# First loads, exponentials by bank and the order of the last tiles in a gated linear-attention and feed-forward kernel

The change has three parts: small loads leave the software DMA queue and the gate column is made by a TensorE transpose; exponentials are done one PSUM bank at a time in the tiles that have little other work behind them; the last tiles are ordered and placed in PSUM differently.

## The chip, the cores and the metric

One core of one Trainium2 chip. The metric is the device time of one execution in microseconds (us). A profile gives the span between first and last instruction, about 2 us less than the time. PE is TensorE's matmul stream, PEld its weight loads, DVE VectorE, ACT ScalarE, POOL GpSimd and SP SyncE; a "q" after a name is its sequencer or DMA queue.

## The reference

```python
# x: [1, 2048, 512] bf16; 32 heads of 16; Dff = 1376
g = sigmoid((x * gate_w).sum(-1, keepdims=True))
q, k, v = heads(x @ wqkv)
pq, pk  = q @ w_phi, k @ w_phi                      # per head, 16 x 16
phi_q   = [softmax(pq), softmax(-pq)]               # 32 features a head; phi_k likewise
kv, z   = phi_k^T v, sum_s phi_k
a       = concat_heads((phi_q kv) / (phi_q z + 1e-6)) @ wo
b       = relu(x @ w1) @ w2
return g * a + (1 - g) * b
```

(B_x is not used; both halves read A_x.)

## The kernel before

A small planner records each engine's instructions with events and turns the events into semaphore waits, so every engine runs in the order of the plan. 16 tiles of 128 rows of x; "H units" are four matmuls each of x @ w1 (128 columns of w1 by 512 rows of x). The loads, in SP's order, and the five small loads on GpSimd's software queue:

```python
for i in range(2):
    p.dma("sp", ... XS[:, 2*i:2*i+2, :] <- xq ...)           # x0i, 256 KB
    load_w1(i)                                               # w10, w11: columns 0..511, 128 KB each
load_w1(2); load_w1(3)                                       # w12, w13
p.dma("sp", ... W1[:, :, 512:DFF] <- B_w1 ...)               # w1r, "the remainder of W1", 864 KB
p.dma("sp", ... WV ...)                                      # 512 KB
p.dma("sp", ... WQKT, transposing ...)                       # wqk, 1 MB
...                                                          # x1..x3, transposing
p.dma("pool", ... WPS <- A_w_phi ...)
for dt in range(NDT):                                        # gate_w as column 1376 of W1
    p.dma("pool", ... W1[:, dt, DFF:DFF+1] <- gate_w ...)
```

The gate's logit is one more output row of the last H unit (`KT - 1`), so that unit needs the gate column. The first units work on w10 to w13; from the fifth on they wait for the remainder. Then come the weight products (`pre`: wqk times the block-diagonal `Wbd`, which DVE builds from w_phi), then the tiles:

```python
def atile(m):        # Q and K features into PSUM banks 0 and 1, then the exponentials
    first = xready(m // 4) + ([f"em{m-1}"] if m else [pc0..pc7])     # both banks read by ACT
    for dt in range(NDT):
        for which, W in ((0, WqP), (1, WkP)): matmul(PS[:, which, :], ...)
    for s, nm in ((0, "ep"), (1, "em")):                             # lastq: by bank
        act(exp, out 128x1024, in PS[:, 0:2, :], scale=+-1)
    ...
nh = [2, 2, 2, 2, 2, 1, 2, 2, 1, 2, 2, 1, 3, 2, 2]                   # H units behind each tile

def nd(m):           # numerators: two banks, 0,1 or 4,5; then divide and DMA-transpose into OT
def finB(m):         # relu(h) @ w2, eleven matmuls, banks 2, 3, 7
def finA(m):         # OT @ wo, four matmuls, bank 6, scaled by g on ACT
...
nd(0); hnext(); gate(); finB(1)
nd(1)
for m in range(NT - 1):
    if m + 2 < NT: nd(m + 2)
    finA(m); comb(m)
    if m + 2 < NT: finB(m + 2)
last(NT - 1)         # tile 15 in two halves
```

The softmax here doesn't subtract the row's maximum and nothing guards it: scores larger than these inputs give would overflow.

## Time and profile before

| | us |
|---|---|
| time, median of three runs | 156.34 (155.41 to 156.79) |
| time, median of six runs, three of them beside the changed kernel | 156.09 (154.95 to 159.93) |
| span of the profiled run | 153.7 |
| PE busy | 146.7 of it (95%), 928 matmuls |
| first H unit on the remainder starts | 10.56 |
| projections of tile 0 start | 20.30 |
| first combine of the last tile, after PE's last matmul slot | 0.73 |

A profile is read here by asking where PE's stream has a hole and what ended it. In the "chain that ended last" each row is start, duration and what; "issue" is time in which the profile shows nothing to wait for. A row of "waits" gives who waited <- for whom, us in all, times, longest. The slot of a 512-column matmul is 0.216 us in this trace; where starts lie further apart there is a hole. The lines are in the prediction.

### The profile page before, as it was taken

The numbers are of one execution on the slowest core, as the hardware profiler recorded it, in microseconds if no ns is written. First come the engines' busy times: TensorE is split into PE (matmuls) and PEld (weight loads), VectorE is DVE, ScalarE is ACT, GpSimd is POOL, SyncE is SP. The second block draws the span as 40 slices with busy tenths as digits, with TensorE's granted clock in tenths as the row PEclk, the third lists the DMA queues.
The fourth block names the chain that finished last, engine by engine and source line by source line (L and its number), as shares of the span: only waits on it lengthen the run. The fifth ranks groups of instructions, "written<-read, shape, count | busy, mean of one in ns | idle before, by whom it ended". The sixth has DMA issues, their size and how long they took to land.

```text
span 153.7 us, 2371 instructions
## 1 busy us (share of the span) xinstructions
PE 146.7 (95%) x928; PEld 72.8 (47%) x928; DVE 90.0 (59%) x147; ACT 79.2 (52%) x122; POOL 55.4 (36%) x62
## 2 busy tenths in 40 slices
PE   5979999999999999999999999999999999999990
PEld 1834644444445444444544445444444444544450
DVE  1600546777668876866868788564545544455523
ACT  3357749788777877887787773111221111111131
POOL 8100007778866866878686653000000000000000
PEclk9999999999999999999999999999999999999999
DMA  4799992963433331533333311433222233233222
GB/s 165 193 320 259 156 237 53 374 145 73 68 68 68 70 61 35 47 68 70 68 75 68 68 27 41 102 72 103 68 68 73 69 87 83 68 93 82 68 68 68
DMA packets 41178, 15.57 MB, mean 101 GB/s; under 512 B 36704, under 2 KB 40432, under 8 KB 41168
## 3 DMA queue, kind: packets, MB, share of 16 engines
q1 hardware_dynamic: 40336, 13.47, 39.7%
q0 software_dynamic: 688, 1.95, 3.9%
q8 instruction: 7, 0.11, 0.3%
q14 instruction: 3, 0.02, 0.1%
q10 hardware_dynamic: 144, 0.01, 0.0%
HBM read 4.41 MB, written 2.10 MB: 42 GB/s over the span
## 4 chain that ended last, share of the span: by engine, by line
PE 82%; DMA 8%; ACT 5%; SPq 2%; DVE 1%; issue 1%; DVEq 0%
PE PS L452 22%; PE PS L257 21%; PE PS L306 18%; PE PS L461 8%; PE PS L359 7%; DMA W<-in_B_w_dram 5%; ACT FM L316 4%; DMA OT<-OTM 4%; PE PS L422 2%; PE PS L381 2%; PE PS L286 1%; SPq L139 1%; SPq L150 1%; ACT TFA L466 0%; ACT HT L272 0%
## 5 line engine op out<-in xcount | busy, mean ns | idle before, releaser
L452 PE MATMUL PS<-W,HT 128*128 128x512 bf16 (+1 forms) x176 | 40.6, 379 | 0.0
L257 PE MATMUL PS<-XT,W 128*128 128x512 bf16 (+1 forms) x160 | 38.0, 379 | 1.0 <-DMA W<-in_B_w_dram 1.0
L316 ACT ACTIVATE FM<-PS 128x1024 bf16<-128x1024 f32 x30 | 29.1, 1021 | 14.3 <-PE PS L306 14.3
L342 POOL TENSOR_TENSOR FM<-FM,SC 128x1024 bf16<-128x1024 bf16 x15 | 29.0, 1930 | 15.1 <-DVE SC L327 15.1
L466 ACT ACTIVATE TFA<-PS,GT 128x512 bf16<-128x512 f32 x15 | 10.3, 688 | 42.9 <-PE PS L461 42.9
L324 DVE TENSOR_REDUCE ZB<-FM 128x64 f32<-128x1024 bf16 x16 | 19.5, 1220 | 19.0 <-ACT FM L316 18.6
L272 ACT ACTIVATE HT<-PS 128x512 bf16<-128x512 f32 (+1 forms) x44 | 24.8, 605 | 8.0 <-PE PS L257 5.1
L452 PEld LDWEIGHTS PS<-W,HT 128*128 128x128 bf16 (+1 forms) x176 | 17.2, 98 | 20.8
L306 PE MATMUL PS<-WqP,XT 128*128 128x512 bf16 x64 | 24.3, 379 | 0.2
L257 PEld LDWEIGHTS PS<-XT,W 128*128 128x128 bf16 (+1 forms) x160 | 15.6, 101 | 18.3 <-DMA W<-in_B_w_dram 1.5
L306 PE MATMUL PS<-WkP,XT 128*128 128x512 bf16 x64 | 24.3, 379 | 0.0
L335 DVE TENSOR_REDUCE ZB<-FM 128x64 f32<-128x1024 bf16 x16 | 18.6, 1164 | 0.0
L347 POOL TENSOR_TENSOR FM<-FM,SC 128x512 bf16<-128x512 bf16 x16 | 16.9, 1057 | 1.3
L472 DVE SCALAR_TENSOR_TENSOR OSB<-PS,OMG,TFA 128x512 bf16<-128x512 f32 x15 | 11.3, 751 | 9.6 <-ACT TFA L466 9.6
L359 PE MATMUL PS<-WV,XT 128*128 128x512 bf16 x64 | 16.4, 378 | 0.0
L461 PE MATMUL PS<-WO,OT 128*128 128x512 bf16 x60 | 15.4, 378 | 0.5 <-DMA OT<-OTM 0.4
L428 DVE RECIPROCAL RDEN<-PS 128x32 f32<-128x32 f32 x16 | 5.7, 357 | 16.8 <-PE PS L422 16.8
L432 DVE TENSOR_TENSOR OTM<-PS,RDEN 128x512 bf16<-128x512 f32 x16 | 11.1, 691 | 0.6
L306 PEld LDWEIGHTS PS<-WqP,XT 128*128 128x128 bf16 x64 | 6.2, 98 | 9.2 <-ACT FM L316 1.6
L306 PEld LDWEIGHTS PS<-WkP,XT 128*128 128x128 bf16 x64 | 6.3, 98 | 7.1
L327 DVE RECIPROCAL SC<-ZB 128x64 f32<-128x64 f32 x16 | 8.8, 553 | 0.5
L369 ACT ACTIVATE VS<-PS 128x512 bf16<-128x512 f32 x14 | 8.5, 604 | 0.0
(57 smaller groups left out, 92.4 us busy)
## 6 DMA issues: line engine op xcount, KB each, us to landing
out_dram<-OSB SPq DMA_DIRECT2D x15, 128.0 KB, 1.9
W<-in_B_w_dram POOLq DMA_DIRECT2D x1, 1280.0 KB, 6.6
W<-in_B_w_dram SPq DMA_DIRECT2D x1, 864.0 KB, 7.0
OT<-in_A_x_dram SPq DMA_DIRECT2D x2, 256.0 KB, 2.9
W<-in_B_w_dram SPq DMA_DIRECT2D x4, 128.0 KB, 4.6
WV<-in_A_wqkv_dram SPq DMA_DIRECT2D x1, 512.0 KB, 7.9
WO<-in_A_wo_dram POOLq DMA_DIRECT2D x1, 512.0 KB, 7.0
PHQ<-FM SPq DMA_TRANSPOSE x16, 2.7
```

The lines of the kernel that those rows point to most:

```text
L257: p.op("pe", lambda e, c=c, kt=kt, M=M, dt=dt, bank=bank: e.matmul(PS[0:M, bank, :], W1[:, dt, kt * P:kt * P + M], XT[:, dt, c * 512:(c + ...
L272: p.op("act", lambda e, c=c, kt=kt, Mr=Mr, bank=bank: e.activation(HT[0:Mr, kt, c * 512:(c + 1) * 512], PS[0:Mr, bank, :], ACT.Relu), afte ...
L306: p.op("pe", lambda e, m=m, dt=dt, which=which, W=W: e.matmul(PS[:, which, :], XT[:, dt, m * P:(m + 1) * P], W[:, dt, :], start=(dt == 0), ...
L316: p.op("act", lambda e, o=fm5[:, :, :, s, :], i=src, s=s: e.activation(o, i, ACT.Exp, scale=(1.0 if s == 0 else -1.0)), after=[f"qk{m}"] + ...
L324: p.op("dve", lambda e, b=b: e.tensor_reduce(ZB[:, b, 64:128], FM[:, b, 1, :].rearrange("p (g f) -> p g f", f=DH), AX.X, ALU.add), after=[ ...
L335: p.op("dve", lambda e, b=b: e.tensor_reduce(ZB[:, b, 0:64], FM[:, b, 0, :].rearrange("p (g f) -> p g f", f=DH), AX.X, ALU.add), after=[f" ...
L342: p.op("pool", lambda e, fk=fk, rk=rk: e.tensor_tensor(fk, fk, rk, ALU.mult), after=[f"rz{m}"], ev=f"pk{m}")
L347: p.op("pool", lambda e, b=b, fq=fq: e.tensor_tensor(fq, fq, SC[:, b, 0:32].unsqueeze(2).to_broadcast([P, H, DH]), ALU.mult), after=[f"sc{ ...
L359: p.op("pe", lambda e, m=m, dt=dt, bank=bank: e.matmul(PS[:, bank, :], XT[:, dt, m * P:(m + 1) * P], WV[:, dt, :], start=(dt == 0), stop=( ...
L452: p.op("pe", lambda e, kt=kt, M=M, m=m, bank=bank: e.matmul(PS[:, bank, :], HT[0:M, kt, m * P:(m + 1) * P], W2[0:M, kt, :], start=(kt == 0 ...
L461: p.op("pe", lambda e, t=t, m=m: e.matmul(PS[:, 6, :], OT[:, t, m * P:(m + 1) * P], WO[:, t, :], start=(t == 0), stop=(t == NDT - 1)), aft ...
L472: p.op("dve", lambda e, m=m, ob=ob: e.scalar_tensor_tensor(out=OSB[:, ob, :], in0=PS[:, BB[m % 3], :], scalar=OMG[:, m:m + 1], in1=TFA[:, ...
```

## The change

Intent: take the small software-queue loads out of the way of the first weights; let the next tile's K projections start when the K bank alone has been read; give the first transposes of OT more time and the last tile a shorter tail. The core of the diff (bank numbers and unchanged context cut):

```diff
+        p.dma("sp", ... GWR[:, :] <- gate_w as 4 x 128 ..., "gwr")          # ahead of w1r
         p.dma("sp", ... W1[:, :, W1C:DFF] ..., "w1r")
         p.dma("sp", ... WV ..., "wv")
+        p.dma("sp", ... WPS <- A_w_phi ..., "wps")                          # behind WV
-        p.dma("pool", ... WPS ...)
-        for dt in range(NDT): p.dma("pool", ... W1[:, dt, DFF:DFF+1] <- gate_w ...)
+        def gatecol():
+            pe.transpose(PS[:, 7, 0:NDT], GWR, IDN[0:NDT, 0:NDT])           # after gwr, idn
+            dve.tensor_copy(W1[:, :, DFF:DFF+1], PS[:, 7, 0:NDT])           # ev gw3
+            if kt == 5: gatecol()                                           # second unit on w1r
-        nh = [2, 2, 2, 2, 2, 1, 2, 2, 1, 2, 2, 1, 3, 2, 2]
+        nh = [2, 2, 2, 2, 1, 2, 2, 1, 2, 2, 1, 2, 3, 1, 2]
+        split = [m for m in range(NT - 1) if nh[m] == 1] + [NT - 1]         # 4, 7, 10, 13, 15
         # split tiles: exp(+), exp(-) of the K bank, then of the Q bank; the next tile
         # does its four K projections first, after "emk", then the four Q ones, after "em"
-            b0 = 4 * (m % 2)
+            b0 = 6 * (m % 2)                                                # numerators
-        BB = [2, 3, 7]
+        BB = [2, 3, 4]                                                      # finB; finA in bank 5
         nd(0)
+        nd(1)
         hnext(); gate()
+        hnext()
         finB(1)
-        nd(1)
-        for m in range(NT - 1): ...
+        for m in range(NT - 2):
+            nd(m + 2); finA(m); comb(m)
+            if m < NT - 3: finB(m + 2)
+        finA(NT - 2, 0); comb(NT - 2)
+        finB(NT - 1)
         last(NT - 1)
```

## The prediction

> **What bounds the kernel now.** I read the busy shares first, then the chain that ended last, then the timelines of single engines where that chain leaves the TensorE. The busy shares:
>
> ```profile
> PE 146.7 (95%) x928; PEld 72.8 (47%) x928; DVE 90.0 (59%) x147; ACT 79.2 (52%) x122; POOL 55.4 (36%) x62
> ```
>
> No other engine comes near PE, and PE is at its own pace: in the chain four 512-column matmuls take 0.86 us and eight take 1.73, 0.216 us each, at a granted clock of 0.998. The change takes no 512-column matmul away, so it can win only where the stream of matmuls has holes, and after the last matmul. I looked for holes by taking each matmul's start less the previous start less the time its columns need (0.216 us for 512). The chain, in order of time, shows the same places:
>
> ```profile
> 3.56 6.96 DMA W<-in_B_w_dram
> 10.52 0.05 issue
> 10.56 5.35 PE PS L257 x24
> ...
> 44.30 1.95 ACT FM L316 x2
> 46.24 0.04 issue
> 46.29 1.90 PE PS L306 x8
> ...
> 96.58 2.47 DMA OT<-OTM
> 99.04 0.14 issue
> 99.18 0.55 PE PS L461 x2
> 99.72 3.19 DMA OT<-OTM
> 102.91 0.05 issue
> 102.96 1.04 PE PS L461 x4
> ...
> 148.33 0.88 PE PS L461 x4
> 149.21 0.02 issue
> 149.23 0.70 ACT TFA L466
> 149.93 0.03 issue
> 149.95 0.59 DVE OSB L472
> 150.54 0.08 issue
> 150.62 0.48 DVE OSB L495
> ```
>
> Columns: start, duration, what. There are four kinds of hole. (1) The remainder of W1 lands at 10.52; the previous matmul's slot ended near 9.40, so PE stands 1.16 us. (2) After tiles 5, 8 and 11, which have one H unit behind them, the next tile's projections wait for both exponentials (1.95 us); three holes of 0.22, 0.66 in all. (3) The first two output projections (L461) wait for the transposes of OT: 0.52 and 0.28, together 0.80. (4) At the end PE stops at 149.89, and the first half of the last tile is combined only at 150.62, because ScalarE and VectorE finish tile 14 first. A further 0.16 before the first tile (weight copies) and the gaps among the early PE transposes are untouched.
>
> **What the Trainium skill says.** "DMA: Bandwidth & Descriptors", section "Queues, rings and completion order": each DMA engine takes the rings that have work in turn, packet by packet. Its section "Specifications" says transfers below 512 B are done by read-modify-write. The trace agrees that small software packets sit among the weight loads: the packet records have 64 packets of 16 bytes (the gate column) spread from about 4.4 to 9.5 us. The loads w12 and w13 (128 KB each) finish, on the mean of their 16 completions, about 1.1 us after their predecessor, where 8 rows of 46 ns per engine would need 0.37; from 4.5 to 6.3 us only about 100 rows of 1 KB start per us, against up to 350 near 10 us. That points at, but does not prove, the software packets. "Perfetto Trace Analysis", section "Optimizing Scalar/DVE Operations", says that breaking up instructions can let work finish sooner where ScalarE is unsaturated but makes bubbles elsewhere: hole (2), with ACT at 52%. "TensorE: Matmul & The Clock Gate", section "Back-to-back issue gap", gives about 216 ns for an isolated 512-column matmul and 131 sustained; this trace shows 216 in the stream, so 131 is not used.
>
> **The change part by part.**
>
> Start. Five software loads go (one of w_phi, four of the gate column: 0.92 and 4 x 0.54 us of GpSimd, beside everything else, worth nothing themselves). Two loads join the SP queue at about 0.4 to 0.5 us of issue each, the gate row ahead of the W1 remainder and w_phi behind WV. Issue is not the limit: the remainder was issued at 3.56, and its first packets moved about 2.8 us later. If the software packets caused the slow stretch, w11 to w13 need about 1.1 us (384 rows x 46 ns / 16) instead of 3; the remainder (512 rows x 76 ns / 16 = 2.4 us) lands near 8.5, before PE wants it at 9.40, and all 1.16 us comes back. The gate column costs one PE transpose, estimated at 0.1 us with its weight load, and one small VectorE copy. But that copy stands behind the four Wbd multiplies in VectorE's order, and these now wait for w_phi behind WV. With w_phi landing about 2 us after the remainder (WV: 512 x 46 / 16 = 1.5, plus 0.5 for its small rows, my choice) and 1.2 us for Wbd and the copy, the gate column is ready 3.2 us after the remainder; the unit that needs it is fourth, 3 x 0.864 + 0.05 = 2.65 after the first. If the remainder is 0.9 early this costs nothing; if it is not, PE waits about 0.5 there. The wqk transpose (landed 15.9) then moves with the queue to 14.5 to 15.4, against a need at about 15.5. Start: +1.05 if it works (chance 0.65), about -0.3 to +0.5 otherwise; mean 0.75.
>
> Exponentials by bank. In tiles 4, 7, 10, 13 two 1024-wide instructions (1.95 us) become four of 512, which took 2.07 us in the one tile that had them. The K bank is free after about 1.05 us; PE has 0.25 + 0.86 + 0.86 = 1.97 us of other work, then 0.86 of K projections before it needs Q, at 2.83 against 2.1. All three holes close: 0.66. ScalarE's load there is 2.07 + 0.60 + 0.60 = 3.3 in a 3.7 us period, VectorE's 3.4, GpSimd's 3.25; all fit, with little room.
>
> Numerator banks and the unit moved. nd(1) goes right behind nd(0), and one more unit goes in before finB(1). From nd(0)'s end to the first output projection there are now 0.25 + 0.86 + 0.86 + 2.38 + 0.25 = 4.6 us of PE work; before it was 3.75, and the data came 4.27 after. For the second it is 8 us. Both holes close: 0.80. The moved unit itself costs nothing: all 33 remain.
>
> Last tiles. With finA(14) ahead of finB(15), tile 14 is combined under 2.4 us of matmuls. After finB(15), ScalarE scales tile 15 (0.22 latency + 0.69) during 0.86 us of last projections, so the first half's combine starts about 0.08 us after PE's end instead of 0.73: 0.65. Risk: finA(14) comes 4.36 us after nd(14), and the transposed data takes about 1.1 (VectorE) + 2.4 = 3.5.
>
> Sum: 0.75 + 0.66 + 0.80 + 0.65 = 2.86; all of it working, 3.16. From 156.34: 153.5, at best 153.2.
>
> **The rivals.** (a) The slow weight loads are not the software packets' doing: the packets still trickle from 7.3 to 9.5 us while the queue runs full (16 engines busy), which speaks against them. Then hole (1) stays, the gate column adds a wait on VectorE, and the time is about 154.5. (b) PE is early, but wqk or the gate column takes over as the wait: about half the start's gain goes, 153.8. (c) The tighter one-unit periods make VectorE or GpSimd the bound for the tiles 12 to 15, and the K V sums wait for normalised K: nothing in the old trace shows PE waiting for L342 though tile periods of 3.76 us occurred; I give it 0.1, and up to 1 us. (d) Nothing but the gaps was hidden anyway: not so for (2) to (4), where PE itself stood, or had ended.
>
> **Range and chances.** The sure part is 2.1 us (1.35%), the start moves it between 1.8 and 3.2. Runs of the kernel before lie from 155.41 to 156.79, so a median is good to some 0.5. I choose 153.4 with 152.4 to 154.9. Over 2% needs about 3.1 us, only the case where everything works: 0.33. Within 2%: 0.65. Slower by over 2%: 0.02, since nothing lengthens PE's stream.
>
> **What would show it.** Start: the wait of L257 for in_B_w gone or shorter, and no new wait for VectorE's W1 copy or for wqk; the first L257 matmul near 9.4. Middle: no wait of PE or its weight loads for the exponentials beyond 0.1 us. Finish: no wait of L461's successor for OT; the combine of the last tile within 0.15 us of the last matmul. Wrong would be: a remainder still landing at 10.5, a wait for the gate column over 0.5 us, or new holes after tile 12.

## The result

The changed kernel takes 154.28 us in the median of six runs (153.79 to 154.42), against 156.09 before. The ratio of the fast runs is 0.9894, with a 95% interval of 0.9849 to 0.9938: about 1% faster, within 2%. Ratios here are the mean time of one kernel's fast runs over that of the other's of the same rounds, so not quite the ratio of the medians quoted. The profiled spans are 152.2 and 153.7 us, both of fast runs.

The busy shares of the changed kernel, the first row of its page:

```profile
PE 145.5 (96%) x929; PEld 72.2 (47%) x929; DVE 90.2 (59%) x148; ACT 79.8 (52%) x130; POOL 52.5 (34%) x57
```

PE is still the bound. The changed kernel's chain that ended last, at its two ends and at two places where there were holes (start, duration, what):

```profile
3.98 6.67 DMA W<-in_B_w_dram
10.64 0.05 issue
10.69 1.03 PE PS L255 x4
11.72 0.11 PE PS L275
11.83 4.42 PE PS L255 x20
...
41.14 0.86 PE PS L255 x4
42.01 1.73 PE PS L318 x8
...
98.22 0.26 PE PS L433 x8
98.48 0.86 PE PS L474 x4
...
148.04 0.89 PE PS L502 x8
148.93 0.29 issue
149.22 0.48 DVE OSB L508
```

L255 are the H units, L275 is the gate column's transpose, L318 the projections, L433 the numerators, L474 the output projections, L502 the last of them, L508 the last combine. Between 20.63 and the end of L502 this chain has PE rows alone: the holes at the exponentials and at the first output projections are gone. At the start nothing is better: the remainder of W1 lands at 10.64 instead of 10.52. The changed kernel's waits, the rows that concern PE's first units:

```profile
PEld PS L255 <- DMA W<-in_B_w_dram: 2.0, 1, 2.0
PE PS L255 <- DMA W<-in_B_w_dram: 1.5, 1, 1.5
PEld PS L255 <- DVE W L278: 0.3, 1, 0.3
```

In this profile PE came to the remainder earlier than before (its last slot ended at 9.06 instead of 9.40) and waited longer: the hole is 1.63 us (1.16 before). The earlier weights are not the reason. As the starts of PE's matmuls show, in both profiles the first 256-column matmuls start 0.21 us apart and then 0.11, so PE runs at half pace at first; the full pace comes where the trace's clock records begin, at 5.29 us here and at 6.47 before. (The PEclk row of the page shows full speed for the time ahead of the first record.) Over all runs these records begin between 4.63 and 7.76. In the five profiles with this very start PE reaches the remainder at 9.06, 9.11, 9.69, 9.93 and 10.02, on both sides of the 9.40 of before.

Where the 1.5 us of span went (hole = start less previous start less slot):

| part | predicted | measured |
|---|---|---|
| start, as start of tile 0 | +0.75 (mean of two outcomes) | -0.33 (20.30 to 20.63) |
| exponentials | +0.66 | +0.66 (three holes of 0.22 gone) |
| first output projections | +0.80 | +0.80 (0.52 and 0.28 gone) |
| tail, last matmul slot to first combine | +0.65 | +0.25 (0.73 to 0.48) |
| sum | 2.86 | 1.38, of 1.5 in the spans |

### The profile page after: what moved, and what is told of

The parts are those of the page before. It is cut to its first block, busy times and chain, and to the rows that moved or that the text cites. A ratio compares the mean times of both kernels' runs of the same rounds, so it can differ in the third digit from the quotient of the medians.

```text
span 152.2 us, 2382 instructions
## 1 busy us (share of the span) xinstructions
PE 145.5 (96%) x929; PEld 72.2 (47%) x929; DVE 90.2 (59%) x148; ACT 79.8 (52%) x130; POOL 52.5 (34%) x57
## 4 chain that ended last, share of the span: by engine, by line
PE 91%; DMA 4%; SPq 2%; issue 0%; DVE 0%; DVEq 0%
PE PS L462 25%; PE PS L255 23%; PE PS L318 18%; PE PS L372 9%; PE PS L474 9%; DMA W<-in_B_w_dram 4%; PE PS L433 3%; PE PS L394 3%; PE PS L291 1%; SPq L140 1%; PE PS L502 1%; SPq L151 1%; DVE OSB L508 0%; DVEq L90 0%; SPq L156 0%
## 5 line engine op out<-in xcount | busy, mean ns | idle before, releaser
L255 PE MATMUL PS<-XT,W 128*128 128x512 bf16 (+1 forms) x160 | 38.1, 379 | 1.5 <-DMA W<-in_B_w_dram 1.5
L329 ACT ACTIVATE FM<-PS 128x1024 bf16<-128x1024 f32 x22 | 21.3, 1021 | 10.1 <-PE PS L318 10.1
L255 PEld LDWEIGHTS PS<-XT,W 128*128 128x128 bf16 (+1 forms) x160 | 15.4, 100 | 18.6 <-DMA W<-in_B_w_dram 2.0
L318 PE MATMUL PS<-WqP,XT 128*128 128x512 bf16 x64 | 22.3, 379 | 0.0
L318 PE MATMUL PS<-WkP,XT 128*128 128x512 bf16 x64 | 22.3, 379 | 0.0
L474 PE MATMUL PS<-WO,OT 128*128 128x512 bf16 x60 | 15.2, 378 | 0.0
L334 ACT ACTIVATE FM<-PS 128x512 bf16<-128x512 f32 x20 | 10.3, 604 | 3.8 <-PE PS L318 3.8
L318 PEld LDWEIGHTS PS<-WkP,XT 128*128 128x128 bf16 x64 | 6.2, 97 | 7.9 <-DVE WkP L296 0.5
L318 PEld LDWEIGHTS PS<-WqP,XT 128*128 128x128 bf16 x64 | 6.3, 98 | 7.4
```

The lines of the kernel that those rows point to most:

```text
L255: p.op("pe", lambda e, c=c, kt=kt, M=M, dt=dt, bank=bank: e.matmul(PS[0:M, bank, :], W1[:, dt, kt * P:kt * P + M], XT[:, dt, c * 512:(c + ...
L318: p.op("pe", lambda e, m=m, dt=dt, which=which, W=(WqP, WkP)[which]: e.matmul(PS[:, which, :], XT[:, dt, m * P:(m + 1) * P], W[:, dt, :], ...
L329: p.op("act", lambda e, o=fm5[:, :, :, s, :], i=src, s=s: e.activation(o, i, ACT.Exp, scale=(1.0 if s == 0 else -1.0)), after=[f"qk{m}"] + ...
L474: p.op("pe", lambda e, t=t, m=m: e.matmul(PS[:, bank, :], OT[:, t, m * P:(m + 1) * P], WO[:, t, :], start=(t == 0), stop=(t == NDT - 1)), ...
```

## The experiments

All kernels gave correct results. "Tile 0" is the start of its projections in that run's profile; "before" in a ratio is the kernel before, run beside it. First the table of times; the slow runs are in the medians and ranges but not in the ratios. By the verdicts on record the change, e4, e6, e7 and e11 are the same as before within 2%, and the others unclear.

| kernel | median us | range | ratio to before | 95% interval | span of profile |
|---|---|---|---|---|---|
| changed | 154.28 | 153.79 to 154.42 | 0.9894 | 0.9849 to 0.9938 | 152.2 |
| e1_old_start | 153.89 | 153.06 to 157.35 | 0.9867 | 0.9796 to 0.9937 | 151.2 |
| e2_gate_row_act | 154.02 | 153.70 to 154.34 | 0.9885 | 0.9831 to 0.9939 | 151.8 |
| e3_w1_split | 153.89 | 153.71 to 154.34 | 0.9878 | 0.9816 to 0.9939 | 152.2 |
| e4_no_exp_split | 155.17 | 154.17 to 157.09 | 0.9962 | 0.9936 to 0.9988 | 153.6 |
| e5_only_start | 157.50 | 157.44 to 158.93 | 1.0114 | 1.0050 to 1.0178 | 156.9 |
| e6_old_finish | 156.88 | 154.76 to 158.95 | 1.0023 | 0.9987 to 1.0059 | 155.2 (slow) |
| e7_hold_wv | 158.05 | 156.01 to 160.56 | 1.0074 | 1.0035 to 1.0112 | 157.9 (slow) |
| e8_front_act | 153.65 | 152.92 to 154.86 | 0.9843 | 0.9788 to 0.9898 | 150.9 |
| e9_old_start_split | 153.38 | 152.40 to 155.59 | 0.9816 | 0.9760 to 0.9872 | 151.7 |
| e10_front_act_again | 153.43 | 152.81 to 153.67 | 0.9824 | 0.9786 to 0.9863 | 150.8 |
| e11_after_again | 154.52 | 154.13 to 156.45 | 0.9897 | 0.9857 to 0.9936 | 152.5 |

e1 to e4 shared one chip (before there: 156.3), e5 to e8 another (156.68), e9 to e11 a third (156.35). A second table is worked out from the semaphore and packet records of each trace. A load is split over 16 DMA engines and has 16 completions; PE waits for the last.

| kernel | w13, last completion | remainder: first / median / last | packets of the remainder over 0.3 us | tile 0 |
|---|---|---|---|---|
| before | 7.94 | 9.21 / 9.52 / 10.52 | 3 | 20.30 |
| e1_old_start | 7.61 | 9.32 / 9.78 / 10.06 | 4 | 19.84 |
| changed | 6.66 | 8.50 / 8.85 / 10.64 | 8 | 20.63 |
| e4_no_exp_split | 6.33 | 8.53 / 9.02 / 11.39 | 17 | 21.38 |
| e5_only_start | 6.26 | 8.28 / 8.84 / 11.02 | 20 | 22.70 |
| e6_old_finish | 6.46 | 8.30 / 8.71 / 10.65 | 9 | 20.64 |
| e11_after_again | 6.49 | 8.38 / 9.04 / 10.97 | 15 | 20.96 |
| e2_gate_row_act | 6.33 | 8.02 / 8.88 / 10.23 | 7 | 20.22 |
| e7_hold_wv | 6.47 | 8.00 / 8.31 / 10.26 | 2 | not comparable |
| e3_w1_split, first half | 6.11 | 7.00 / 7.64 / 9.51 | 10 | 20.65 |
| e8_front_act, first half | 6.07 | 6.80 / 7.07 / 7.68 | 3 | 19.21 |
| e10_front_act_again, first half | 5.99 | 6.71 / 7.13 / 8.22 | 6 | 19.19 |
| e9_old_start_split, first half | 8.59 | 8.14 / 8.27 / 9.60 | 0 | 20.20 |

**Does the new start lose, and do the other parts win?** e1 is the changed kernel with the old start.

```diff
-        p.dma("sp", ... GWR ...); p.dma("sp", ... WPS ...); gatecol()
+        p.dma("pool", ... WPS ...); for dt: p.dma("pool", ... W1[:, dt, DFF:DFF+1] ...)
```

> The changed kernel with the old start: w_phi and the gate column come over the software queue again, no gate row, no PE transpose. Theory (the start lost 0.33 us, the other parts won 2.1): the first L255-type matmul after the early ones starts at 10.56 as before, the eight projections of tile 0 near 20.3 instead of 20.63, span 151.85 or so against 152.2. Rival (the new start is no loss by itself, its late W1 remainder was a chance of that one profile): tile 0 no earlier than 20.6 and a time equal to or above the changed kernel's 154.28.

Measured: span 151.2, tile 0 at 19.84. From its chain:

```profile
3.55 6.51 DMA W<-in_B_w_dram
10.06 0.04 issue
10.11 5.35 PE PS L258 x24
...
19.84 1.89 PE PS L321 x8
```

The remainder landed at 10.06, 0.46 earlier than in the profile of before with the same loads, so the landing itself scatters by half a microsecond. The other parts gave 0.66 and 0.80 here too, and the tail 0.61 (0.12 left of 0.73); with 0.46 at the start that is 2.53 of the 2.5 us between the spans. In time e1 and the changed kernel cannot be told apart (intervals overlap widely), so the profiles, not the times, say that the new start is no gain.

e5 is the complement, the kernel before with the new start alone.

```diff
+        GWR, WPS on SP's queue, gatecol() as in the change; everything after the start as before
```

> The kernel before with the new start alone (gate row and w_phi on SP's queue, gate column by PE transpose). Theory (the start is no gain): the projections of tile 0 between 20.2 and 21.4, where the three profiles so far of this start had 20.63, 21.38 and (gate row elsewhere) 20.22, against 20.30 before; span 153.6 to 154.8; the holes of 0.22 us at tiles 6, 9, 12 and of 0.52 and 0.28 at the first output projections are all there again. Rival (the new start alone gains, and was masked by its neighbours): span under 153.2.

Measured: slower than before, 1.0114 with an interval of 1.0050 to 1.0178; tile 0 at 22.70, far beyond the range expected. The three holes of 0.22 us and the first one at the output projections (0.55) are there, the second of those is not; but in this profile most of the time lost is in the start, and in a way that I had not thought of: the granted clock. This is PEclk in the page of e5, tenths of full clock in 40 slices of the span:

```profile
PEclk9995999999999999999999999999999999999998
```

And the same execution in stretches of 3.4 us (busy time and number of instructions per engine, then clock):

```profile
8.90:12.30 3.40, 1.51 (x7) 0.51 (x7) 0.00 (x0) 1.98 (x5) 0.00 (x0) 1.00 1.19 194
12.30:15.70 3.40, 3.31 (x8) 1.33 (x8) 0.98 (x5) 1.11 (x3) 0.00 (x0) 0.50 1.21 271
```

PE was idle for over half of the first stretch, waiting for the remainder (last completion 11.02), and in the next it ran at half clock: 8 matmul records in 3.4 us, where full clock has room for 15. (The traces from this second chip lack single matmul records here and there, seen as gaps of exactly one slot of 0.216; they are not counted as holes.) The clock records of the trace give 0.5 from 12.33 to 15.74, that is 3.41 us. The page "TensorE: Matmul & The Clock Gate" of the Trainium skill, section "What's actually happening", describes an activity window of 3413 ns that runs free of the kernel; this trace agrees with the length. The hole is 1.96 us here and 1.16 before. A window is lost in e7's profile (a slow run) too: a hole of 2.60 us, PE busy for 0.97 of the 3.41 us from 12.50 to 15.91, then 0.5 from 15.91 to 19.32. The changed kernel had a hole of 1.63 with PE busy for 1.94 of the window from 8.71 to 12.12, and kept the full clock; so did e4 and e11 with 1.41 and 1.09. If it is the busy share of a window that counts, the limit lies here between 1.50 and 1.94 of 3.41 us; these traces show it no finer.

The lost window does not explain e5's times, though. The record has the mean granted clock of each run: 0.985 for the profiled one, which is the slowest (158.93), and 1.0, 0.998 and 0.993 for the others (157.44 to 157.53). A lost window takes half of 3.41 us out of 157, which is 0.011, so none of these three lost one, and they still lie 1.5 us above the mean of the fast runs of before (155.99). They were not profiled, so why the new start alone costs that much stays open.

**Why is the remainder not earlier?** The second table answers half. Without the software loads w13 is complete at 6.0 to 6.7 in all ten profiles of the new start and its variants; with them at 7.6, 7.9 and 8.6. So the loads on the software queue did hold up the first weights, by 1.3 us, as the prediction supposed (in e8 and e10 the same small loads go over ScalarE's queue and w13 is complete at 6.07 and 5.99). In the kernel before, PE hardly waited for these weights: ahead of the remainder, it has only 0.05 us of hole at w12. Most engines pass the gain on: the first and median completions of the remainder are 0.7 us earlier. The last is not. I first suspected the gate row, just ahead of the remainder, which is only four packets of 256 bytes and so can make at most four engines late.

```diff
-        p.dma("sp",  ... GWR ...)
+        p.dma("act", ... GWR ...)       # first thing on ScalarE's queue
```

> The changed kernel, with the gate row issued first thing from ScalarE's queue instead of ahead of the W1 remainder in SP's. Theory S (the gate row, which goes over four engines only, makes those four late): the completions of the W1 remainder lose their stragglers (last near 9.5 instead of 10.64), PE resumes near 9.5, wqk lands near 15.8 and becomes the next wait; tile 0 near 19.8, span near 151.4. Rival H (some of the 16 engines are slow in reading the W1 remainder whatever stands before it): last completion still at 10.3 or later, tile 0 within 0.3 us of 20.63.

Measured: the last completion is at 10.23 and the stragglers remain (five completions from 9.4 to 10.2), tile 0 at 20.22. That is neither 9.5 nor unchanged. With the gate row ahead, five profiles have 10.64, 11.39, 11.02, 10.65 and 10.97, without it two have 10.23 and 10.26: the row may well cost some 0.5, but it is not the main cause, and five against two profiles on three chips do not settle its share.

Then I suspected the traffic of the engines that finish early and go on into the next loads.

```diff
+        p.wait("sp", ["w1r"])
         p.dma("sp", ... WV ...)         # gate row on ScalarE's queue, as in e2
```

> The changed kernel with the gate row on ScalarE's queue and the load of WV held back until the W1 remainder has landed. A test of why 4 to 5 of the 16 completions of the remainder come 1 to 2 us late. Theory B (the engines that finish early go on into WV, w_phi and the transposes and take the others' bandwidth): without that traffic the last completion comes at 9.2 or earlier and all 16 lie within 1.3 us. Theory E (some engines are slow by themselves, or the reads of these rows are): last completion still at 10 or later, spread about 2 us. The time is not of interest: WV, w_phi and wqk come later, tile 0 near 21.5.

Measured: fifteen completions lie between 8.00 and 8.64, and one comes at 10.26. Neither theory is right as put: holding WV back may have pulled in most of the field (within 1.3 us, as theory B asked), but the last is still beyond 10. The packet records say what happened, here as start in us, size, duration in ns:

```
last packets of the remainder, in intervals of 0.25 us from 8.0: 16, 7, 4, 3, 4, 4, 3, 3, then none
from 8.32 on: one packet every 0.07 us, each taking 72 ns
longest of all: 1142 ns, started at 6.18
```

From 8.3 to 9.9 a single engine moves its packets one after another at the ordinary 72 ns; it is not slow, it is late, and the stretch also has one packet of 1142 ns early in the load. The last column but one of the table counts such long packets: there are 3 or 4 in the remainder with the old start and 7 to 20 with the new one in front of WV (but 2 in e7, where WV was held). In w10 to w13 there are 12 and 8 of them with the old start and 0 to 10 with the new one. So such packets come in either case; with the new start more of them fall into the load for which PE waits. That they are what makes an engine late is likely and not shown: the records name neither the engine nor the cause of a packet of 0.3 to 1.1 us. PE's wait is shown to be for the last one to five of 16 completions; that bandwidth is not what they lack is shown for e7 alone.

**What lies behind that wait?** e3 splits the remainder, so that the first three units wait for less.

```diff
-        p.dma("sp", ... W1[:, :, 512:DFF] ..., "w1r")
+        p.dma("sp", ... W1[:, :, 512:896] ..., "w1r")       # units 4, 5, 6
+        p.dma("sp", ... W1[:, :, 896:DFF] ..., "w1s")       # the others
```

> The changed kernel with the W1 remainder in two loads, columns 512 to 895 (needed by the first three units) ahead of 896 to 1375. Theory (the wait at 10.6 is for the landing of the whole remainder, and the next limit is close behind): PE resumes near 9.3 and the 1.5 us hole closes, but wqk, which landed at 16.6, is now what the weight products wait for, since PE reaches them at about 15.6; tile 0 near 20.4, gain 0.2 to 0.4 us only. Rival (no further limit): tile 0 near 19.3, gain 1.3 us.

Measured: PE resumes at 9.55, as expected, and tile 0 starts at 20.65, no gain at all. The next limit is there, but it is not wqk. From e3's waits:

```profile
PEld PS L258 <- DVE W L281: 1.4, 1, 1.4
PE PS L258 <- DVE W L281: 0.9, 1, 0.9
```

L281 is DVE's copy of the gate column. In DVE's order it stands behind the four Wbd multiplies, which wait for w_phi, which the change put behind WV. This wait (a hole of 1.1 us by the starts) was in the prediction as a condition: free if the remainder is early, about 0.5 if not. In the changed kernel the late remainder hides most of it (0.3 in PEld, and no hole in PE).

e8 removes both: the gate row and w_phi go first on ScalarE's queue, the remainder is split, and the gate column is made ahead of the first unit on it.

```diff
-        p.dma("sp",  ... GWR ...); p.dma("sp",  ... WPS ...)
+        p.dma("act", ... GWR ...); p.dma("act", ... WPS ...)
+        w1r split as in e3
-            if kt == 5: gatecol()
+            if kt == 4: gatecol()
```

> A version meant to beat both: the changed kernel with gate row and w_phi issued first on ScalarE's queue, the W1 remainder in two loads (columns 512 to 895 first), and the gate column transposed ahead of the first of these units. Theory (with the wait for the whole remainder and the wait for w_phi behind WV both gone, the next limit is wqk, landing near 15.7 to 16): PE resumes near 9.6, no wait for the gate column, perhaps a wait of up to 0.5 for wqk; tile 0 near 19.5, span near 151.1, time near 153.0. Rival (early loads on a second queue slow x and the first W1 blocks as the software loads did): the last of the first W1 blocks lands at 7.5 or later and tile 0 is no earlier than 20.2.

Measured: tile 0 at 19.21, span 150.9, ratio 0.9843. From e8's waits, all that PE's first units and the weight products still wait for:

```profile
PEld PS L294 <- DMA PHQ<-in_A_wqkv_dram: 0.3, 1, 0.3
```

That is wqk, expected at up to 0.5; it holds the weight loads and leaves no hole in PE. The chain that ended last runs through PE from its first transposes at 3.60 on, so the start is now PE's own work, its stretch at half pace included. It is 1.42 us better than the changed kernel's. Run again beside the changed kernel on a third chip:

> e8_front_act once more, on the chip of e9 and e11, for the comparison: tile 0 near 19.2, span near 150.9, no wait for the gate column, a wait of about 0.3 for wqk. If its first W1 half lands after 9.6 this time, the start is as scattered as that of the changed kernel.

> The changed kernel once more: a further sample of its start on this chip. Theory (single late engines hold the whole remainder): last completion of the remainder between 10.2 and 11.4, a hole in PE of 1.3 to 2.0 us, tile 0 between 20.2 and 21.4, span 151.8 to 153[...].

Measured: e10 has tile 0 at 19.19 and span 150.8, a median of 153.43 and a ratio of 0.9824 (0.9786 to 0.9863); the changed kernel beside it 154.52 and 0.9897, tile 0 at 20.96 with the remainder at 10.97 and a hole of 1.09 (below the 1.3 expected). The profiles repeat closely. Part of that is chance: the clock records begin at 6.37 and 6.21, and PE reaches the remainder's first half at 9.28 and 9.22. Had the full pace come as late as in e4 (10.02), tile 0 would be some 0.7 us later (an estimate from these starts). In time the version gains 0.7% over the change by the medians (153.43 against 154.52 on one chip); a gain of over 2% over the kernel before is not established for it either.

Last: is leaving the software queue worth anything, once nobody waits for the whole remainder?

```diff
         e1_old_start, with w1r split as in e3
```

> The changed kernel with the old start (w_phi and gate column over the software queue) and the W1 remainder in two loads as in e8_front_act. Asks whether leaving the software queue is worth anything once nobody waits for the whole remainder. Theory (it is the split and the early gate column that pay; the software packets delay the first W1 blocks by 1.3 us but little else): PE resumes near 9.6 with a hole under 0.4, no wait for the gate column (it lands near 9.8, needed near 12), tile 0 at 19.3 to 19.7, within 0.5 us of e8_front_act's 19.21. Rival (the software queue costs a microsecond as the change supposed): tile 0 at 20.0 or later.

Measured: the profile has tile 0 at 20.20, so my theory failed by its own number. From its chain:

```profile
5.96 10.50 DMA PHQ<-in_A_wqkv_dram
16.46 0.05 issue
16.51 1.07 PE PS L297 x16
```

PE first waited for late x and W1 blocks (holes of 0.87 and 0.66 us before 8; w13 was complete only at 8.59), so it reached the remainder's first half at 10.25 instead of e10's 9.22; wqk then landed at 16.46, a microsecond later than in e10 (15.46), which made a hole of 0.22. In that profile the software loads cost 1.0 us. The times do not confirm it: medians 153.38 and 153.43. The five fast runs of e9 range over 1.8 us (the sixth was slow) and the six of e10 over 0.9, and e9's profiled run (153.53) is an ordinary one. What the software queue costs on average, once the remainder is split, stays open.

**The other two parts.** e4 takes the exponentials by bank away again, in tiles 4, 7, 10 and 13.

```diff
-        split = [m for m in range(NT - 1) if nh[m] == 1] + [NT - 1]
+        split = [NT - 1]
```

> The changed kernel with the exponentials by bank only in the last tile, as before; tiles 4, 7, 10 and 13 keep one unit. Theory: four holes of 0.22 us come back at the projections of tiles 5, 8, 11 and 14, span +0.88 (153.1). Rival (the holes are hidden by later slack): span within 0.2 of 152.2. Its start is that of the changed kernel, so it is also a second sample of the landing of the W1 remainder: near 10.6 if that is typical.

Measured: four holes of 0.22, 0.22, 0.22 and 0.27 us, at the projections of tiles 5, 8, 11 and 14. The row of its waits:

```profile
PEld PS L318 <- ACT FM L329: 2.2, 4, 0.6
```

In the changed kernel there is no such row. The span is 153.6, of which 0.75 is a later start (remainder at 11.39), 0.93 the holes, and the tail gave back 0.36 (0.48 to 0.12). So the part is worth what was predicted, hole by hole.

e6 puts nd(1) and the last finB back in their old order and leaves banks and units as changed.

```diff
-        nd(0); nd(1); hnext(); gate(); hnext(); finB(1)
+        nd(0); hnext(); gate(); hnext(); finB(1); nd(1)
-        finA(NT - 2, 0); comb(NT - 2); finB(NT - 1)
+        finB(NT - 1); finA(NT - 2, 0); comb(NT - 2)
```

> The changed kernel with nd(1) back behind finB(1) and the last finB back ahead of the output projection of tile 14; banks and the moved H unit stay as changed. Theory: the first output projection still has no hole (the moved unit covers it), the second has one of about 0.3 us, and the last combine starts 0.7 us after PE's end instead of 0.3 or less; span +0.8 to +1.0 from these two over a run of the same start. Rival (the order does not matter, the banks made the gain): no hole and no longer tail.

Measured: no hole at the first output projection, as expected. At the second the hole is 2.05 us instead of 0.3. From e6's chain:

```profile
99.38 4.44 DMA OT<-OTM
103.82 0.05 issue
103.87 1.04 PE PS L474 x4
```

The transpose took 4.44 us from issue to landing, where the median in every profile here is 2.4. The packet records show one packet of 16 KB on the instruction queue (q8 in the page) from 101.27 to 102.76, in the middle of it. In the profile of before such a packet starts at 100.13, within the transpose that took 3.19. All 13 traces together settle how often this goes together: of 208 transposes of OT, the 167 that such a packet overlaps by less than 0.3 us took at most 2.51 us; of the other 41, in fast and slow runs alike, 30 took 2.7 to 4.4 and 11 at most 2.47. So every long transpose had such a packet in it, though not every packet made one long. I have not removed the packet.

This changes what the second hole means. With 2.42 us the transpose of before (issued at 99.72) would have landed at 102.14, ahead of PE's need at 102.67, and that of e6 at 101.80, where PE needed it at 101.82: no hole in either, by this estimate. In e5, which has the order of before, it took 2.41 and there was no hole. So the 0.28 of before and the 2.05 of e6 come with a lengthened transpose; what nd(1) right behind nd(0) buys is the slack to hide one. At the end e6 starts its first combine 1.07 us after PE's last slot, 0.59 later than the changed kernel.

## Why the prediction was right or wrong

The time (154.28) lies within 152.4 to 154.9, and within 2% was the likeliest outcome. The range was wide enough to hold the failure of its start (rival (a), 154.5), and that is what happened, so the number alone does not speak for the mechanism: two of its four terms came out, the start failed, and the tail got 0.25 of 0.65. Of the signs of being wrong that it named, the first came true (a remainder still landing at 10.5: 10.64). By its steps:

- **What bounds the kernel**: right. PE did stay the bound, and the gains came from the holes found in the trace of before. PE's half pace at the start (until 6.47 in that trace) was not seen; the clock of 0.998 does not show it.
- **Start**: wrong. The step that failed is "the remainder ... lands near 8.5, before PE wants it at 9.40, and all 1.16 us comes back". Its first half held: w13 is complete 1.3 us earlier. But the sum treated a load as if its 16 engines ended together. The remainder's median completion moved from 9.52 to 8.85, its last from 10.52 to 10.64, and PE waits for the last. With the transpose's 0.20 that is the later tile 0 (20.30 to 20.63). Nor is 9.40 a fixed need: with this start it lay between 9.06 and 10.02, with the beginning of the full pace. I had the spread of completions before me (9.21 to 10.52 before) and used only a mean rate.
- **Gate column**: the transpose was taken at 0.1 and cost PE 0.20 (0.10 ahead of it and 0.10 behind). The wait for DVE's copy was named with its cause; it was 0.3 in PEld here, with no hole in PE, and 1.1 once the remainder was early enough (e3). The estimate of "2 us after the remainder" for w_phi was near: 12.40, which is 1.76 after. But "if the remainder is 0.9 early this costs nothing" was wrong: in e3, where its first half lands at 9.51, w_phi still lands at 12.42.
- **Rival (a)** gave the outcome (hole stays, 154.5) for a reason that the runs refute: the slow first blocks are the software packets' doing. Rival (b) was half right: behind the remainder the gate column stands next (e3); wqk, in e8 and e10, holds the weight loads by 0.3 to 0.4 us and PE by at most 0.04. Rival (c) did not occur: no new hole after tile 12.
- **Exponentials by bank**: right, 0.66, confirmed by e4.
- **Numerator order and the moved unit**: right, 0.80 in the profiles of before and after. The first hole (0.52) is closed by the moved unit: e5, in the old order, has it and e6, with the unit moved and the order back, does not. The second (0.28) rests on a transpose that took 3.19 us instead of 2.42, which stands in the prediction's own lines and was not asked about.
- **Last tiles**: right in mechanism, mis-sized. Of 0.65 the changed kernel got 0.25, because VectorE starts its combine late. Its sequencer's wait ends at 148.80, with the inputs of the first half there, and the combine starts 0.42 us later (the chain shows 0.29 of that as "issue", after the end of all matmuls). In e1, e4 and e9 the same step takes 0.04 and the first combine comes 0.12 after PE's last slot, as predicted (0.08). The delay goes with the program and not with the single run: 0.41 to 0.42 stands in the eight traces in which VectorE has 191 recorded instructions ahead of this combine (the changed kernel, e11, e2, e3, e6, e7, e8 and e10), and in none of the five with 187, 188 or 190. e6's tail, too, is the expected 0.7 with this delay on top. What it is stays open; adding or removing one VectorE instruction, which would test it, was not run.

The working added up to 2.86 us; the start came out 1.08 below its term and the tail 0.40 below its own, which leaves 1.38, close to the 1.5 between the two spans. The medians differ by 1.8, within their scatter.

## What to carry to other kernels

A wait on a DMA is a wait for the slowest of its 16 engines: read the spread of its completions before you count on a faster queue, and cut the load so that the first consumer waits for the least (e8 and e10). Where engines run in plan order, follow each moved load to everything queued behind its consumer: w_phi behind WV held the gate column only because DVE's copy stood behind Wbd. And a hole in PE can cost more than its length: in the profiles of e5 and e7 half the clock for the next 3.41 us. Last, compare several executions before you explain a start: when PE reaches full pace moved by 3 us from run to run here.

## What the Trainium skill lacked or had wrong

- "DMA: Bandwidth & Descriptors", section "Queues, rings and completion order", names the round robin between rings, and the runs agree that small software packets delay others (w13 complete at 7.6 to 8.6 with them, 6.0 to 6.7 without). It has no figure for the spread between the completions of one load: 1.3 us before, 2.1 to 2.9 with the changed kernel's start.
- "Runtime: NRT & Kernel Launch", section "Instruction fetch mechanics", says that instructions are refilled in blocks of 16 KiB by DMA and that the cost is mostly hidden. The records have such packets, seven in each execution, of 0.9 to 2.4 us each. What it does not have is their price for a DMA transpose under way: of 41 transposes that one overlapped, 30 took 2.7 to 4.4 us, while the 167 others took at most 2.51 (not tested by removal).
- "TensorE: Matmul & The Clock Gate", section "Back-to-back issue gap", gives 131 ns per 512-column matmul as sustained and 216 as isolated; in all these traces the sustained stream has 216.
- "TensorE: Matmul & The Clock Gate", section "Why this matters for your kernels", warns of gaps of more than about 3 us; in e5 one hole of 1.96 us, in a stretch of 3.40 us with PE busy for 1.51, was followed by 3.41 us at a clock of 0.5, and in e7 one of 2.60 us likewise.
- "TensorE: Matmul & The Clock Gate", "Part 4: PE-mode transpose", has no figure for a small transpose between matmuls: a 4 x 128 one cost the stream 0.20 us.
